# Setting the assumed lengths of ACT's units and TensorE's small jobs in a kernel that orders its own instructions

## The chip, the cores and the metric

The kernel runs on one core of a Trainium2 chip. The metric is the device time of one execution in microseconds (us). In the views below PE is TensorE's matmuls, PEld its weight loads, ACT is ScalarE, DVE is VectorE, POOL is GpSimd; L345 is line 345 of the kernel.

## The reference, cut to what matters

The program is an attention with pooled keys, and a two-layer network with a GELU of the quick kind behind it, on 49152 rows of 128:

```python
kv_pool = kv.reshape(B, H // 4, 4, W // 4, 4, C).mean(axis=(2, 4))
k = v = kv_pool.reshape(B, -1, C) @ w_sr           # 768 keys for each of 4 batches
s = (1.0 / np.sqrt(C)) * (q @ k.transpose(0, 2, 1))
a = softmax(s)                                       # exp of 49152 x 768 numbers
x = (a @ v).reshape(B * S, 128)
h = x @ w_in                                         # 128 -> 2048
g = h * (1.0 / (1.0 + np.exp(-1.702 * h)))           # 49152 x 2048 numbers
out = g @ w_out                                      # 2048 -> 128
```

## The kernel before

The kernel takes no scheduler's help: its Python code emits the instructions, and each engine runs its own in exactly that order. The work is cut into 700 *units*. A unit is a **fill** on PE (three matmuls of 512 columns into three PSUM banks) and one ACT instruction (exp or GELU) that turns those banks into a result in SBUF. Two sets of three banks alternate. Later, PE **drains** the results: for attention by matmuls of 129 columns (L345, twelve for a unit on average), for the network by output matmuls of 512 columns (L520, three for a unit). The results wait in a ring of 102 slots, three to a unit. Besides, PE has small jobs: pooling, making keys and values, transposes ("turns").

While it emits, the code keeps a reckoning of time in units of one 512-column matmul. `now` is PE's time, `end[n]` the time at which ACT ends unit n. Between two fills it emits drains and jobs as long as they fit ahead of the next fill, by these lengths:

```python
FIXED, CHUNK, SWITCH, HANDOVER, EVACUATE, LATE = 0.33, 1.975, 6.0, 1.0, 4.5, 1.0
COST = {pool_chunk: (2.5, 2.0), key_chunk: (0.7, 2.0), ...}    # PE's length, then time until the bank is free
SMALL, TURN = 0.26, 5.5                                        # SMALL: one 129-column matmul

def fill(p):
    ...                                                        # emits the fill and the ACT instruction
    begin = max(now + HANDOVER / 2, end[p - 1] if p else 0.0)
    ...                                                        # (cut) a switch of table adds SWITCH
    end.append(begin + FIXED + CHUNK * len(part))

for n in range(len(seq)):
    fill(n + 2)
    while True:
        room = room_ahead()                                    # free slots of the ring
        limit = end[-1] - K - HANDOVER                         # K = 3; (cut) no limit at the very end
        ...                                                    # small jobs, if they fit
        if not source:
            if todo_early and all(...made...):                 # parked exp units are all there
                source = todo_early
            else:
                source = todo
        ...
        cost = K * SMALL if kind == "a" else 1.0
        ...                                                    # (cut) drains whose results are not there yet
        start = now if source is todo_early else max(now, end[needs] + HANDOVER)
        ...                                                    # (cut) the first drain of a group waits for its bank
        if start + cost > limit and not (room < 2 * K + 1 or (room < 4 * K and start == now)):
            break                                              # (cut) the slot is full
        now = start + cost
        (drain_attn if kind == "a" else drain_moe)(i, c)
```

`room` counts the free slots of the ring. When fewer than 12 are free, a drain whose results are ready is emitted whether it fits or not, and when fewer than 7 are free, any drain is. I call this a **forced** drain, and "slot" with a length in us below means the PE work between the ends of two fills. Four of the attention groups ("early" or parked) have their exp made by DVE; their 24 chunks occupy a fixed part of the ring.

The softmax here doesn't subtract the row's maximum and nothing guards it: scores larger than these inputs give would overflow.

## Time and profile before

| what | value |
|---|---|
| time, three runs | 972.28, 972.39, 972.58 us |
| profiled execution | 971.47 us, span 969.7 us |
| PE busy, ACT busy | 946.0, 946.4 us (98% each) |
| first full ACT unit starts | 12.7 us |
| last ACT unit ends | 963.8 us |

A group's row in the profile reads: line, engine, operation, output and input with shapes, count, then busy time and mean length in ns of one, then the idle time just before them and what ended it. The groups of PE that the change's reckoning is about, by shape:

```profile
L520 PE MATMUL banks<-ag,w_out_sb 128*128 128x512 bf16 x1517 | 410.0, 379 | 1.8 <-ACT ag L515 0.5 <-DVE o_sb L528 0.2
L345 PE MATMUL banks<-v,ag 128*128 128x129 bf16 x2304 | 162.9, 220 | 0.4 <-DVE v L158 0.3
L134 PE MATMUL banks<-sum,x 128*128 128x32 bf16 x192 | 6.7, 177 | 0.1
```

The mean of one (379, 220, 177 ns) is not what a matmul costs, since each starts long before the previous record ends. What it costs is the distance from start to start. Some matmul records are missing in this trace (1517 of 1536 at L520).

### The profile page before, as it was taken

How to read it: one execution, taken by the hardware profiler on the slowest of the kernel's cores; microseconds unless marked ns; L12 is line 12 of the kernel's file. 1: busy time of each engine (PE TensorE's matmuls, PEld its weight loads, DVE VectorE, ACT ScalarE, POOL GpSimd, SP SyncE). 2: the span in 40 equal slices, each digit the busy share in tenths (PEclk: the TensorE clock that was granted, in tenths of full speed). 3: DMA queues.
4: the chain of work that ended last, by engine and by line, in shares of the span. 5: the costliest groups of instructions: out<-in, count | busy, mean ns of one | idle time of the engine just before them, and what ended most of it. 6: DMA issues, size and time to landing. Idle time of an engine off the chain costs nothing.

```text
span 969.7 us, 15127 instructions
## 1 busy us (share of the span) xinstructions
PE 946.0 (98%) x6244; PEld 504.7 (52%) x6359; DVE 344.0 (35%) x734; ACT 946.4 (98%) x705; POOL 65.7 (7%) x113
## 2 busy tenths in 40 slices
PE   7899999999999999999999999999999999999997
PEld 3567777544444444454445777754444444444443
DVE  4444433201477778777602333311111011011010
ACT  4999999999999999999999999999999999999997
POOL 3100100340000232000000000000000000000000
PEclk9999999999999999999999999999999999999999
DMA  9899841999862698224348994652222222222222
GB/s 182 161 201 148 110 96 34 108 147 172 162 130 44 103 149 110 41 34 76 57 81 132 182 174 106 131 120 40 37 44 39 38 44 34 43 34 40 37 33 43
DMA packets 354164, 89.66 MB, mean 92 GB/s; under 512 B 328048, under 2 KB 351728, under 8 KB 353776
## 3 DMA queue, kind: packets, MB, share of 16 engines
q1 hardware_dynamic: 323936, 56.06, 33.7%
q0 software_dynamic: 29104, 32.51, 22.6%
q8 instruction: 49, 0.80, 0.3%
q10 hardware_dynamic: 1056, 0.13, 0.1%
q14 instruction: 19, 0.16, 0.1%
HBM read 52.49 MB, written 45.88 MB: 101 GB/s over the span
## 4 chain that ended last, share of the span: by engine, by line
ACT 48%; PE 47%; DMA 3%; DVE 1%; issue 1%; POOL 0%; POOLq 0%
ACT ag L515 36%; PE banks L513 17%; PE banks L520 17%; ACT ag L336 13%; PE banks L345 6%; PE banks L334 5%; DMA qT<-q_bf 2%; DMA x<-in_q_dram 1%; DVE qT L230 1%; PE banks L382 1%; PE banks L424 0%; PE banks L224 0%; DVE o_sb L528 0%; ACT L515 0%; PE banks L134 0%
## 5 line engine op out<-in xcount | busy, mean ns | idle before, releaser
L515 ACT ACTIVATE ag<-banks 128x1536 bf16<-128x1536 f32 x512 | 690.0, 1543 | 1.6 <-PE banks L513 1.5
L513 PE MATMUL banks<-x,w_in_sb 128*128 128x512 bf16 x1484 | 411.2, 379 | 2.9
L520 PE MATMUL banks<-ag,w_out_sb 128*128 128x512 bf16 x1517 | 410.0, 379 | 1.8 <-ACT ag L515 0.5
L336 ACT ACTIVATE ag<-banks 128x1536 bf16<-128x1536 f32 (+1 forms) x188 | 250.6, 1445 | 12.2 <-PE banks L334 11.7
L520 PEld LDWEIGHTS <-w_out_sb 128*128 128x128 bf16 x1536 | 149.6, 97 | 181.7 <-issue 1.6
L513 PEld LDWEIGHTS <-w_in_sb 128*128 128x128 bf16 x1536 | 147.6, 97 | 176.5 <-issue 20.1
L528 DVE STREAM_TRANSPOSE o_sb<-banks 128x512 f32<-128x512 f32 x96 | 68.7, 716 | 398.8 <-PE banks L520 386.5
L345 PEld LDWEIGHTS <-ag 128*128 128x128 bf16 x2304 | 146.4, 98 | 45.4 <-issue 1.2
L345 PE MATMUL banks<-v,ag 128*128 128x129 bf16 x2304 | 162.9, 220 | 0.4 <-DVE v L158 0.3
L334 PE MATMUL banks<-qT,kT 128*128 128x512 bf16 x508 | 146.9, 379 | 9.3 <-ACT ag L336 4.8
L354 DVE RECIPROCAL rec<-banks 128x3 f32<-128x3 f32 x128 | 23.0, 180 | 132.9 <-PE banks L345 132.7
L409 DVE SCALAR_TENSOR_TENSOR ea<-ea,eb 128x512 f32<-128x512 f32 x96 | 65.9, 687 | 2.8
L334 PEld LDWEIGHTS <-kT 128*128 128x128 bf16 x552 | 47.4, 98 | 36.2 <-issue 4.5
L362 DVE TENSOR_TENSOR x<-banks,rec 128x384 bf16<-128x384 f32 x104 | 57.9, 557 | 3.6
L166 POOL DMA_DIRECT2D kvs<-in_kv_dram x32 | 40.4, 1319 | 15.8 <-DMA kvs<-in_kv_dram 11.6
L449 POOL MEMSET gate_tile<- 1x8 f32 x38 | 4.0, 106 | 461.9 <-DVE gate_tile L448 461.9
L398 DVE TENSOR_SCALAR ea<-banks 128x512 f32<-128x512 f32 x24 | 16.6, 691 | 30.1 <-PE banks L382 30.1
L411 DVE SCALAR_TENSOR_TENSOR ag<-ea,ee 128x512 bf16<-128x512 f32 x24 | 16.5, 686 | 1.0
L404 DVE SCALAR_TENSOR_TENSOR eb<-eb,ea 128x512 f32<-128x512 f32 x24 | 16.5, 688 | 0.7
L362 DVE TENSOR_TENSOR xt<-banks,rec 128x384 bf16<-128x384 f32 x24 | 13.4, 557 | 0.8
L230 DVE COPY qT<-banks 128x512 bf16<-128x512 bf16 x15 | 9.8, 686 | 4.8 <-PE banks L224 4.6
L426 DVE COPY x<-banks 128x768 bf16<-128x768 bf16 x12 | 6.7, 557 | 12.0 <-PE banks L424 11.9
(65 smaller groups left out, 154.5 us busy)
## 6 DMA issues: line engine op xcount, KB each, us to landing
out_dram<-o_sb SPq DMA_DIRECT2D x382, 64.0 KB, 2.0
kvs<-in_kv_dram POOLq DMA_DIRECT2D x32, 384.0 KB, 6.2
q_bf<-in_q_dram POOLq DMA_DIRECT2D x20, 512.0 KB, 7.3
x_bf<-x SPq DMA_DIRECT2D x13, 768.0 KB, 5.7
x<-in_kv_dram POOLq DMA_DIRECT2D x12, 512.0 KB, 12.3
x<-in_q_dram POOLq DMA_DIRECT2D x3, 512.0 KB, 20.6
w_in_sb<-in_moe_w_in_dram POOLq DMA_DIRECT2D x1, 512.0 KB, 5.1
w_out_sb<-in_moe_w_out_dram POOLq DMA_DIRECT2D x1, 512.0 KB, 6.6
```

The source lines that it names most:

```text
L166: nc.gpsimd.dma_start(out=kv_sums[b][:, i2], in_=kv_p[b, i, w, :, i2], **({"accum_op": ADD} if n else {}))
L230: nc.vector.tensor_copy(dst, src)
L334: nc.tensor.matmul(ps[:, k, :], kTs[i // GB][:, jc * 128:(jc + 1) * 128], rhs, start=True, stop=True)
L336: nc.scalar.activation(place([("a",) + c for c in chunks]), ps, AF.Exp, scale=scale)
L345: nc.tensor.matmul(av_of[u][:, k * (C + 1):(k + 1) * (C + 1)], weights(("a", i, jc))[:, o:o + T], vs[i // GB][:, jc, 0:C + 1], start=(jc = ...
L354: nc.vector.reciprocal(rec, ps[:, :, C])
L362: nc.vector.tensor_tensor(to, ps[:, :, 0:C], rec.unsqueeze(2).broadcast_to([128, TS, C]), MUL)
L409: nc.vector.scalar_tensor_tensor(a, a, COEFFS[k], b, ADD, MUL)
L513: nc.tensor.matmul(ps[:, k, :], w_in_sb[:, fc * 128:(fc + 1) * 128], x[:, g % (4 * XS) * G:(g % (4 * XS) + 1) * G], start=True, stop=True)
L515: nc.scalar.activation(place([("m",) + c for c in chunks]), ps, AF.Gelu_apprx_sigmoid)
L520: nc.tensor.matmul(o_of[g], w_out_sb[:, fc, :], weights(("m", g, fc)), start=(fc == 0), stop=(fc == FCH - 1))
L528: nc.vector.transpose(o_sb, o_of.pop(g))
```

## The change

Its intent is to put the lengths that an earlier trace shows in place of the old estimates. No instruction is added, removed or altered; only the order in which they are emitted follows from these numbers.

```diff
-    FIXED, CHUNK, SWITCH, HANDOVER, EVACUATE, LATE = 0.33, 1.975, 6.0, 1.0, 4.5, 1.0
-    COST = {pool_chunk: (2.5, 2.0), key_chunk: (0.7, 2.0), value_chunk: (0.7, 2.0),
-            transpose_q: (1.2, 4.0), early_fill: (1.0, 5.5), key_and_value: (1.0, 3.0),
-            transpose_pooled: (1.5, 3.0), make_k: (1.0, 3.0), make_v: (1.5, 3.0), turn: (1.5, 3.5)}
+    FIXED, CHUNK, SWITCH, HANDOVER, EVACUATE, LATE = 0.295, 1.978, 6.0, 1.0, 4.5, 1.0
+    COST = {pool_chunk: (1.9, 2.6), key_chunk: (0.3, 2.4), value_chunk: (0.3, 2.4),
+            transpose_q: (1.05, 4.2), early_fill: (1.0, 5.5), key_and_value: (0.55, 3.5),
+            transpose_pooled: (0.9, 3.6), make_k: (0.8, 3.2), make_v: (0.8, 3.7), turn: (1.55, 3.5)}
```

## The prediction

> **What bounds the kernel now.** I read the page's busy shares first, then ACT's waits, then ACT's groups in chosen stretches, then TensorE (PE) in order of time.
>
> ```profile
> PE 946.0 (98%) x6244; PEld 504.7 (52%) x6359; DVE 344.0 (35%) x734; ACT 946.4 (98%) x705; POOL 65.7 (7%) x113
> ```
>
> Both PE and ACT look full. The PE figure flatters: a matmul's record lasts 379 ns while the next starts after 216. ACT's figure also needs care, as shown below. ACT makes 700 units (up to three banks, 128x1536) of exp or GELU; nothing else can make them, except 24 chunks of exp on DVE. The waits of ACT over the whole run:
>
> ```profile
> ACT ag L336 <- PE banks L334: 11.7, 8, 3.9
> ACT qT L228 <- PE banks L224: 2.9, 1, 2.9
> ACT ag L515 <- PE banks L513: 1.5, 2, 1.3
> ```
>
> In order of time, almost all of the 11.7 us lies before 23 us (the first loads); the rest is 1.4 us near 39, 1.0 near 72.7 and 1.5 us near 425 to 428. So open idle time worth winning after the start is about 4 us. But some loss is not shown as idle. These are ACT's rows in five stretches, one answer each: 101 to 148, 152 to 230, 525 to 612, 641 to 803 and 850 to 960 us:
>
> ```profile
> L336 ACT ACTIVATE ag<-banks 128x1536 bf16<-128x1536 f32 x36 | 49.0, 1459 | 0.0
> L515 ACT ACTIVATE ag<-banks 128x1536 bf16<-128x1536 f32 x58 | 78.5, 1461 | 0.0
> L336 ACT ACTIVATE ag<-banks 128x1536 bf16<-128x1536 f32 x66 | 89.6, 1466 | 0.0
> L515 ACT ACTIVATE ag<-banks 128x1536 bf16<-128x1536 f32 x121 | 163.5, 1459 | 0.0
> L515 ACT ACTIVATE ag<-banks 128x1536 bf16<-128x1536 f32 x83 | 111.9, 1781 | 0.0
> ```
>
> The same instruction takes 1781 ns in the last row and about 1460 in the others. The records overlap, so I take the pace as (busy - one mean) / (count - 1): 1.358, 1.352, 1.356, 1.350 and 1.343 us per unit. My reading: 1.343 us is ACT's own pace; there its next unit is issued some 0.33 us early and queues behind the previous one, which the record includes. Where the mean is 1460 nothing queues: ACT starts each unit just when PE has filled the banks, and PE sets the pace, 7 to 15 ns per unit too slow, without any idle being shown.
>
> PE's pace is what the emitting code decides, because PE runs strictly in the order in which the code emits. Between two fills it places as much other work ("drains" and small jobs) as it believes fits in one ACT unit. Near 427 us it placed far too much:
>
> ```profile
> 424.66 0.81 PE L513 MATMUL banks<-x,w_in_sb 128*128 128x512 bf16 x2
> ...
> 425.31 1.18 PE L345 MATMUL banks<-v,ag 128*128 128x129 bf16 x18
> ...
> 426.33 1.24 PE L520 MATMUL banks<-ag,w_out_sb 128*128 128x512 bf16 x5
> ...
> 427.41 0.81 PE L513 MATMUL banks<-x,w_in_sb 128*128 128x512 bf16 x3
> ...
> 428.25 4.15 ACT L515 ACTIVATE ag<-banks 128x1536 bf16<-128x1536 f32 x3 [1.30 <-PE banks L513]
> ```
>
> Between two fills stand 18 attention matmuls and 5 output matmuls (one fill record is missing), 2.1 us of work; the ring of result slots was nearly full, and the code's rule for that case overrides the limit.
>
> **What the Trainium skill says.** "TensorE: Matmul & The Clock Gate", section "Wait — 56ns, not 53.3ns?", gives start-to-start times of warm matmuls of 215.7 ns at 512 columns, 55.6 at 128, and a floor of 25 for small ones. This trace agrees: x3 of 512 columns last 0.81 us, less one record of 0.379, over two steps: 0.215; x12 of 129 columns last 0.84, less 0.220, over 11: 0.056; sixteen 32-column ones last 0.55, less 0.177, over 15: 0.025. "Perfetto Trace Analysis", section "DVE / Act Engine Instruction", says the start that is reported is when an instruction leaves the execution queue for the ALUs; the 1781 ns means here speak against that for queued units, and I go by the trace. "ScalarE: Activation LUTs", section "What ACT_TABLE_LOAD costs", gives 186 ns + 0.833 per element less 93 of overlap, from which I estimate 1.373 us for 1536 elements; measured is 1.343, which decides.
>
> **The change part by part.** It adds and removes no instruction. The numbers steer the order alone; one unit of them is a 512-column matmul, 0.2157 us.
>
> (1) ACT's unit goes from 0.33 + 3 x 1.975 = 6.255 to 0.295 + 3 x 1.978 = 6.229, that is from 1.3492 to 1.3436 us. The new value is ACT's measured pace; the old one lets PE take 5.6 ns too much per unit, whenever there is a backlog of drains. That matches the 1.350 of the stretch from 641 us. In attention a triple of 129-column matmuls is reckoned at 0.78 but takes 3 x 0.0567 / 0.2157 = 0.789; 3.255 of drains is then 3.29, 6.29 in all, 1.357 us, as measured at 525 (1.356). After: 3.229 becomes 3.265, 1.351; this error of 1% stays, as the change leaves it alone.
>
> (2) The small jobs get shorter: sixteen pooling matmuls 16 x 0.0251 / 0.2157 = 1.86 (2.5 before, 1.9 now), two of 128 columns 0.52 (1.0, now 0.55), a turn of six 1.55 (1.5, now 1.55). Their sum with the time until the bank is free is about the same, so bank releases are not reckoned earlier. Effect: more drains beside a pooling job.
>
> The program order of both kernels, counted from fill to fill with the durations above, shows this. The first 27 slots are the same. Units 464 to 584 (641 to 803 us): 31 slots with four output matmuls become 28, mean work 1.3495 to 1.3441. Units 376 to 444 (second attention part): 1.3571 to 1.3522. Units 54 to 100 (first): 1.3558 to 1.3523. The backlog lasts longer: units 585 to 614, 1.3014 to 1.3445. The slots of 1.88 and 2.75 us near 425 us vanish; in their place one of 2.18 (27 attention matmuls, unit 309), one of 1.73 (321), and at 347 one of 1.98 instead of 1.63.
>
> Gains, counted in ACT units:
> - 641 to 816 us: 130 units at 1.350 become 1.344: 130 x 0.006 = 0.8 us.
> - 152 to 230 us: 57 units, of 0.009 lost about 0.007 comes back: 0.4.
> - Attention, 76 to 148 and 525 to 612 us: 47 + 65 units x 0.0057 = 0.6.
> - 232 to 418 us: 138 units, pace 1.344: 0.15 at most; I take 0.1.
> - The stall near 425: ends of ACT units are there 1.69 and 2.75 us apart instead of 1.343 each, 1.75 us lost, plus 0.17 at unit 347 (484 us). A slot costs its length less 1.343 less the lead that ACT has. In before the two slots exceeded by 1.94 and cost 1.75, the 1.63 one exceeded by 0.29 and cost 0.17; so the lead was 0.12 to 0.2, say 0.15. After: 2.18 costs 0.68, 1.73 costs 0.23, 1.98 costs 0.48: 1.4. Gain 1.92 - 1.4 = 0.5; with more lead (0.33, as late in the run) the gain is 1.1. I take 0.7.
> - 20 to 100 us: one slot of 1.66 becomes 1.33 (0.2 us lost at 48 us), but behind it stands a transposing transfer of q that lands at 71.8 and holds PE 1.1 us; what is won before is mostly waited out there. I take 0.1.
>
> Sum: 0.8 + 0.4 + 0.6 + 0.1 + 0.7 + 0.1 = 2.7 us. The start (23 us) and the tail after ACT's last unit (963.8 to 969.7) do not change. 972.4 - 2.7 = 969.7.
>
> **Rivals.** (a) A large gain, over 2%: it would need 19 us. ACT alone needs 700 units x 1.343 = 940 (a little less for eight shorter units), plus three table loads, plus 12.7 us until its first full unit and 6 of tail: about 961. What is left to win is some 10 us, of which 6 are start. I rule it out. (b) No gain: the lead is spent elsewhere. For it: the forced slots move rather than vanish, and the q transfer swallows early gains; against it: the pace in the 400 units is steady and set by the budget alone. It would leave 971.5 to 972.4. (c) A loss: with shorter job costs the code packs slots of 1.56 us (16 pooling and 9 attention matmuls) where before 1.39 stood, and holds the backlog longer, so the ring fills and other forced slots arise. For it: 2.18 at unit 309; against: the neighbours of the 1.56 slots hold 0.93 to 1.32. It could cost 1 to 2 us net, giving 973 to 974. (d) Transfers: loads issue where PE and DVE reach their gates, moved by a few units; a q transfer that lands 1 us later costs 1 us.
>
> **Range and chances.** The pace part (1.9 us) is firm to about 0.6; the forced slots and the transfers by about 1 each. I put 8 in 10 on 968.3 to 971.3. The runs of before lie within 0.3 us of each other, and 2% is 19.4 us: faster by over 2% 0.01, within 2% 0.98, slower 0.01.
>
> **What would show it.** ACT's pace from 641 to 803 falls from 1.350 to 1.343 to 1.345, its mean rises above 1459 ns; in attention it falls to about 1.351 with the mean still near 1460. The 1.3 us wait near 428 is gone, and one of 0.5 to 0.7 stands near 431. The q wait near 72 us stays around 1. Wrong would be: a pace unchanged at 1.350, new waits of ACT over 1 us, or PE waiting for DVE to free an accumulator.

## The result, and the profile after

The changed kernel took 968.87 us (median of 4 runs, 968.77 to 969.10); the kernel before took 972.49 (median of 4). The ratio is 0.9961, with an interval of 0.9944 to 0.9978. The predicted time was 969.7 with a range of 968.3 to 971.3. All outputs are right.

The two traces differ less than these medians: spans of 969.7 and 967.3 us, 2.4 us apart. In a later job both kernels ran on one chip in five rounds: 971.51 (median of 9) and 969.20 (median of 5), ratio 0.9973, 2.3 us apart. The earlier timed runs of before lay about 1 us above its own profiled execution (972.3 to 973.6 against 971.47). Those runs left no trace, so where that microsecond went stays open; I explain the 2.4 us that the traces hold.

The page's busy shares of the changed kernel, which tell next to nothing:

```profile
PE 950.7 (98%) x6359; PEld 505.5 (52%) x6359; DVE 345.2 (36%) x734; ACT 944.5 (98%) x705; POOL 65.7 (7%) x113
```

PE's count rises by 115 only because no record is missing in this trace. ACT's waits over the whole run, the three longest rows (engine, tile and line that waited, what it waited for, us in total, times, longest):

```profile
ACT ag L336 <- PE banks L334: 12.0, 8, 3.8
ACT qT L228 <- PE banks L224: 2.9, 1, 2.9
ACT ag L515 <- PE banks L513: 1.0, 2, 0.7
```

The waits fell by only 0.2 us in sum (11.7 + 1.5 to 12.0 + 1.0). A reader who judges by shown idle time would expect nothing. ACT's rows in the same five stretches as in the prediction show where the rest is:

```profile
L336 ACT ACTIVATE ag<-banks 128x1536 bf16<-128x1536 f32 x36 | 48.7, 1474 | 0.0
L515 ACT ACTIVATE ag<-banks 128x1536 bf16<-128x1536 f32 x59 | 79.5, 1470 | 0.0
L336 ACT ACTIVATE ag<-banks 128x1536 bf16<-128x1536 f32 x66 | 89.3, 1487 | 0.0
L515 ACT ACTIVATE ag<-banks 128x1536 bf16<-128x1536 f32 x122 | 164.1, 1483 | 0.0
L515 ACT ACTIVATE ag<-banks 128x1536 bf16<-128x1536 f32 x83 | 111.7, 1747 | 0.0
```

By (busy - one mean) / (count - 1):

| stretch, us | work | before | after |
|---|---|---|---|
| 101 to 148 | attention | 1.358 | 1.349 |
| 152 to 230 | end of attention's drains, then network | 1.352 | 1.345 |
| 525 to 612 | attention | 1.356 | 1.351 |
| 641 to 803 | network | 1.350 | 1.344 |
| 850 to 960 | network, no backlog | 1.343 | 1.341 |

The rows give busy time to 0.1 us, so each pace is good to 0.001 or 0.002; the difference in the last row is of that size. In the fourth stretch 122 units fit where 121 did.

The forced slot moved. PE's and ACT's instructions of the changed kernel in order of time (start, length, engine, line and operation, count, and in brackets the idle time before it and who ended it):

```profile
428.92 0.81 PE L513 MATMUL banks<-x,w_in_sb 128*128 128x512 bf16 x3
429.56 1.69 PE L345 MATMUL banks<-v,ag 128*128 128x129 bf16 x27
431.10 0.81 PE L513 MATMUL banks<-x,w_in_sb 128*128 128x512 bf16 x3
...
431.94 4.32 ACT L515 ACTIVATE ag<-banks 128x1536 bf16<-128x1536 f32 x3 [0.65 <-PE banks L513]
```

The wait of 1.30 us at 428 is gone, and one of 0.65 us stands at 432, behind 27 attention matmuls in one slot, as the program order had shown.

To account for every unit, I took from both traces the times at which ACT ends its units, and counted as loss what the distances exceed 1.3435 us, ACT's own pace. The shorter units of the start are counted at full length too, which makes the first row's loss some 4.2 us too small in both kernels and leaves its gain as it is. The losses are good to about 0.02 us. Units count from 0; a range a to b here and below runs from the end of unit a to the end of unit b:

| units | loss before, us | loss after, us | gain | gain predicted |
|---|---|---|---|---|
| 0 to 20, the start | 3.61 | 3.45 | 0.16 | 0 |
| 20 to 54 (40 to 88 us) | 1.89 | 1.89 | 0.00 | 0.1 |
| 54 to 101 and 376 to 446, attention | 4.30 | 3.63 | 0.67 | 0.6 |
| 101 to 262 | 0.67 | 0.13 | 0.54 | 0.5 |
| 262 to 350, forced slots | 1.97 | 1.79 | 0.18 | 0.7 |
| 446 to 590 | 0.88 | 0.09 | 0.79 | 0.8 |
| 590 to the end | 0.00 | 0.03 | -0.03 | 0 |

The attention row holds two loads of ACT's tables in both kernels; the range from 350 to 376, with the third, is left out: it loses 1.41 us in both. The sum is 2.3 of the 2.4 us.

### The profile page after: what moved, and what is told of

Its sections match the earlier page's. It is cut to its first block, busy times and chain, and to the rows that moved or that the text cites. A ratio compares the mean times of both kernels' runs of the same rounds, so it can differ in the third digit from the quotient of the medians.

```text
span 967.3 us, 15236 instructions
## 1 busy us (share of the span) xinstructions
PE 950.7 (98%) x6359; PEld 505.5 (52%) x6359; DVE 345.2 (36%) x734; ACT 944.5 (98%) x705; POOL 65.7 (7%) x113
## 4 chain that ended last, share of the span: by engine, by line
PE 50%; ACT 45%; DMA 3%; DVE 1%; issue 0%; POOL 0%; ACTq 0%; POOLq 0%
ACT ag L515 36%; PE banks L520 17%; PE banks L513 17%; ACT ag L336 9%; PE banks L345 7%; PE banks L334 7%; DMA qT<-q_bf 2%; DMA x<-in_q_dram 1%; DVE qT L230 1%; PE banks L382 1%; PE banks L224 0%; PE banks L424 0%; DVE o_sb L528 0%; ACT L515 0%; PE banks L134 0%
## 5 line engine op out<-in xcount | busy, mean ns | idle before, releaser
L515 ACT ACTIVATE ag<-banks 128x1536 bf16<-128x1536 f32 x512 | 688.9, 1539 | 1.2 <-PE banks L513 1.0
L334 PE MATMUL banks<-qT,kT 128*128 128x512 bf16 x552 | 149.7, 379 | 6.9 <-ACT ag L336 4.5
```

The source lines that it names most:

```text
L334: nc.tensor.matmul(ps[:, k, :], kTs[i // GB][:, jc * 128:(jc + 1) * 128], rhs, start=True, stop=True)
L515: nc.scalar.activation(place([("m",) + c for c in chunks]), ps, AF.Gelu_apprx_sigmoid)
```

## The experiments

All ran in two jobs of five rounds, on two chips, each with its own runs of the kernel before: 971.51 us in the first, 971.50 in the second (medians of 9). I therefore compare across the two jobs too, and give the change to 969.20, the changed kernel of the first job. The theory is that two separate things happen: PE's pace in backlogged stretches is the budget that the code gives it, and drains forced by a nearly full ring cost extra. Building the kept kernels again, without the chip, with a line that logs every drain gives the number of forced drains in each; I call that the emission log. It counts 14 in the kernel before (6 of them parked ones) and 22 in the changed one (5 parked).

### The changed kernel again

> The changed kernel itself, beside the others on one chip. Both theories: 3.6 us faster than before (3.0 to 4.0).

It took 969.20 us (968.89 to 969.73), ratio 0.9973 (0.9960 to 0.9985): 2.3 us faster than before, under the range that I had written down from the first result. Its trace repeats the first one: the losses of the rows above from unit 54 on agree within 0.02 us. The start and the wait for a transfer near 72 us vary more, by some 0.2 us each.

### Only ACT's unit

```diff
 # the kernel before, with
-    FIXED, CHUNK, SWITCH, HANDOVER, EVACUATE, LATE = 0.33, 1.975, 6.0, 1.0, 4.5, 1.0
+    FIXED, CHUNK, SWITCH, HANDOVER, EVACUATE, LATE = 0.295, 1.978, 6.0, 1.0, 4.5, 1.0
```

> Only ACT's unit is changed (6.255 to 6.229 matmul lengths), the small jobs keep the old costs. Program order from fill to fill: mean work in units 464 to 584 falls 1.3495 to 1.3441 us, as in the full change, but the two forced slots at units 304 and 305 (1.88 and 2.75 us) stay, with new ones of 1.73 and 1.71. My theory (two separate parts: the pace, and the forced slots): about 1.3 us faster than before (0.9 to 1.9), ACT's pace from 641 to 803 us 1.344, the wait of 1.3 us near 427 us still there. Rival (the small jobs' costs give all of the gain): at most 0.3 us faster and the pace still 1.350. Rival (luck of transfers): any value, with the same pace as before.

It took 970.64 us, ratio 0.9992 (0.9979 to 1.0005): 0.9 us by the medians, at the lower edge of what I expected, and not clear of noise as a time. The trace is clear. ACT's row from 641 to 803 us, and its longest wait in the network:

```profile
L515 ACT ACTIVATE ag<-banks 128x1536 bf16<-128x1536 f32 x121 | 162.8, 1477 | 0.0
```
```profile
ACT ag L515 <- PE banks L513: 1.8, 3, 1.3
```

The pace is (162.8 - 1.48) / 120 = 1.344, that of the full change, while the wait of 1.3 us is still there. From unit 446 to 590 it loses 0.17 us (before 0.88), but from 262 to 350 it loses 2.91 (before 1.97): less PE work per slot fills the ring sooner, and more is forced. The emission log bears this out: the ring is down to nine free slots at unit 224 (in before at 286, in the changed kernel at 309), and 46 drains are forced instead of 14. Part of the pace's gain is paid back there.

### Only the small jobs

```diff
 # the changed kernel, with
-    FIXED, CHUNK, SWITCH, HANDOVER, EVACUATE, LATE = 0.295, 1.978, 6.0, 1.0, 4.5, 1.0
+    FIXED, CHUNK, SWITCH, HANDOVER, EVACUATE, LATE = 0.33, 1.975, 6.0, 1.0, 4.5, 1.0
```

> Only the small jobs' costs are changed, ACT's unit stays 6.255. Program order: mean work in units 464 to 584 is 1.3495 as before; of the forced slots one of 2.10 us is left at unit 304 instead of 1.88 and 2.75. My theory: about 1.5 us faster than before (1.0 to 2.2), all of it near 425 us (about 1.2) and near 48 and 484 us, pace from 641 to 803 still 1.350. Rival (the unit alone matters): no gain. The two halves should add up to the whole change within 0.7 us.

It took 970.75 us, ratio 0.9989 (0.9977 to 1.0002): 0.8 us, less than I expected. Again the same two views, row and wait:

```profile
L515 ACT ACTIVATE ag<-banks 128x1536 bf16<-128x1536 f32 x121 | 163.5, 1457 | 0.0
```
```profile
ACT ag L515 <- PE banks L513: 0.8, 2, 0.5
```

The pace is (163.5 - 1.46) / 120 = 1.350, as before: the jobs' costs do nothing for it. From 262 to 350 it loses 0.65 us, 1.3 less than before, which is the gain that I expected there; the emission log has 7 forced drains. It lost 0.8 us between units 160 and 200, where before lost 0.04 and where I had expected nothing; the trace shows, among others, one output matmul that waited 0.4 us for DVE to empty the bank of a key job just before it (PE's wait between 215 and 300 us):

```profile
PE banks L520 <- DVE kT L186: 0.4, 1, 0.4
```

I had not looked for that in the program order. The halves sum to 1.6 us by the medians, against 2.3 for both, just within the 0.7 that I had allowed. From unit 54 on the traces give 0.9 and 0.5 against 2.2. What is missing is not in the forced slots: from 262 to 350 the unit alone loses 0.9 and the jobs alone win 1.3, 0.4 together, where both at once win 0.2. It lies between units 101 and 262: the unit alone wins 0.35 there, the jobs alone lose 0.70, but both at once win 0.55. So the jobs' new costs run into that loss only with the old unit; why, stays open.

### Parked drains only while the ring has room

```diff
 # the changed kernel, with
-                if todo_early and all((i, jc) in made ...
+                if todo_early and room >= 6 * K and all((i, jc) in made ...
```

> The changed kernel with one more condition: the parked exp units are drained only while at least 18 result slots are free. Theory: the forced slots come from draining those when fewer than 12 slots are free, since they free no slot; with the condition no slot over 1.6 us is left in the program order between units 102 and 356, the waits of ACT near 432 and 484 us vanish (0.72 + 0.17 + 0.47 us lost there in the changed kernel), so 1.3 us faster than the changed kernel (0.8 to 1.6), about 4.9 faster than before. Rival (the waits there come from DVE or from the q transfer at 431 us): the waits stay, same time as the changed kernel within 0.3 us.

It took 967.78 us, ratio 0.9960 (0.9946 to 0.9973), 1.4 us faster than the changed kernel beside it; 3.7 faster than before, where I had named 4.9 from the larger gap of the first measurement. All of ACT's waits that are left in this kernel:

```profile
ACT ag L336 <- PE banks L334: 11.8, 8, 3.8
ACT qT L228 <- PE banks L224: 3.1, 1, 3.1
ACT L228 <- PEq L719: 0.7, 1, 0.7
```

No row of L515 is left: the network's waits are gone. From unit 300 to 350 the loss falls from 1.57 us to 0.10. The emission log shows why: in the changed kernel, in the long slot of unit 309, nine slots were free, and five triples of *parked* attention drains were forced. The parked chunks keep their slots until the last is drained, so such a drain frees nothing, and output drains had to be forced right after (two in the next slot). With the gate, at least 12 slots stay free and not one drain is forced. The rival (DVE or a transfer of q at 431 us makes the wait) falls.

### The measured length of a 129-column matmul

```diff
 # the changed kernel, with
-    SMALL, TURN = 0.26, 5.5
+    SMALL, TURN = 0.263, 5.5
```

> The changed kernel with one more constant set to its measured length: a 129-column matmul reckoned at 0.263 instead of 0.26. Program order: mean work in the attention units 54 to 100 falls 1.3523 to 1.3451, 376 to 444 1.3522 to 1.3448; but a forced slot of 3.77 us stands at unit 305 instead of 2.18 and 1.73. Theory: attention wins 0.6 us or so (pace from 525 to 612 us 1.346), the forced slot loses about 0.7 more than the two of the changed kernel, 1.63 at 347 gives 0.35 back: the same as the changed kernel within 0.5 us. Rival (pace is all that counts): 0.8 us faster than the changed kernel.

It took 968.77 us, ratio 0.9976 (0.9964 to 0.9989): the same as the changed kernel. ACT's row in the stretch of 525 to 612 us, and its wait in the network:

```profile
L336 ACT ACTIVATE ag<-banks 128x1536 bf16<-128x1536 f32 x66 | 88.9, 1607 | 0.0
```
```profile
ACT ag L515 <- PE banks L513: 2.0, 1, 2.0
```

The mean of 1607 ns says that units now queue in front of ACT, and the pace is (88.9 - 1.61) / 65 = 1.343: attention is at ACT's own pace too. What this wins (0.7 us in the two attention ranges) went into a forced slot of 3.77 us: 2.08 us lost at units 300 to 310, 1.03 in the changed kernel. The 0.4 us between the medians is within the spread of the runs, so it is this slot, not the time, that speaks against the rival (pace is all that counts).

### Both

```diff
 # the changed kernel, with
-    SMALL, TURN = 0.26, 5.5
+    SMALL, TURN = 0.263, 5.5
-                if todo_early and all((i, jc) in made ...
+                if todo_early and room >= 6 * K and all((i, jc) in made ...
```

> Both: 0.263 and the parked exp drained only while 18 slots are free. Program order: attention 1.345, largest slot between units 102 and 356 is 1.73. Theory: the gains add: 2.2 us faster than the changed kernel (1.6 to 2.6), about 5.8 faster than before. Rival (late stretches take back what is won, since PE then is the bound overall): no more than 1.4 us faster than the changed kernel.

It took 966.59 us (966.38 to 967.19), ratio 0.9952 (0.9938 to 0.9965): 4.9 us faster than before, and 2.6 faster than the changed kernel, at the upper edge of what was expected. It beats both kernels. The 5.8 us against before that I had named came from the larger gap of the first measurement. ACT's row from 525 to 612 us:

```profile
L336 ACT ACTIVATE ag<-banks 128x1536 bf16<-128x1536 f32 x66 | 88.9, 1619 | 0.0
```

The gain in attention is as in the run before (1.343 per unit), and from 262 to 350 only 0.03 us is lost. Beyond 88 us, its three table loads aside (1.42 us each), it loses about 0.2 us in all against ACT's own pace.

### The budget too long, and too short

```diff
 # the changed kernel, with FIXED at 0.347 (unit_6281) or 0.28 (unit_6214)
-    FIXED, CHUNK, SWITCH, HANDOVER, EVACUATE, LATE = 0.295, 1.978, 6.0, 1.0, 4.5, 1.0
+    FIXED, CHUNK, SWITCH, HANDOVER, EVACUATE, LATE = 0.347, 1.978, 6.0, 1.0, 4.5, 1.0
```

> The changed kernel with ACT's unit reckoned 0.052 too long (6.281 matmul lengths, 1.3548 us) instead of right. Program order: attention 1.3668 and 1.3620, units 122 to 164 1.3544, units 464 to 584 only 1.3263 because the backlog is used up sooner; forced slots 1.73 and 1.66. Theory (PE's pace is set by the budget): the stretches 101 to 148 and 525 to 612 us run at 1.365 and 1.361 a unit; in all 3 to 4 us slower than the changed kernel. Rival (the drop of budget had no effect of its own): the same as the changed kernel within 0.5 us.

It took 972.58 us, ratio 1.0015 (1.0003 to 1.0028), 3.4 us slower than the changed kernel. The row from 525 to 612 us:

```profile
L336 ACT ACTIVATE ag<-banks 128x1536 bf16<-128x1536 f32 x65 | 88.6, 1460 | 0.1
```

That is (88.6 - 1.46) / 64 = 1.362 a unit, as expected. From 101 to 148 us it is 1.358 where I had named 1.365, a miss: before had 1.358 there too. Over the whole range from unit 54 to 101 it does lose more than before (2.38 us against 1.99); why this stretch did not follow its program order stays open. The rival (the budget has no effect of its own) falls.

> ACT's unit reckoned 0.015 too short (6.214, 1.3404 us). Program order: all stretches 1.340 to 1.349, so PE no longer sets the pace outside attention, but the drains fall behind and the forced slot at unit 305 grows to 3.77 us, with 1.80 at 347. Theory: the optimum of the budget is at ACT's pace; here 0 to 1 us slower than the changed kernel, with one ACT wait of about 2.2 us near 430 us. Rival (shorter is always better): 0.5 us faster.

It took 969.53 us, ratio 0.9981 (0.9969 to 0.9994), 0.3 us slower than the changed kernel, with one wait of 2.0 us from the slot of 3.77 us. ACT's row from 525 to 612 us:

```profile
L336 ACT ACTIVATE ag<-banks 128x1536 bf16<-128x1536 f32 x65 | 87.8, 1519 | 0.0
```

Attention ran faster, (87.8 - 1.52) / 64 = 1.348, and the ring took it back, 2.08 us at units 300 to 310. The 0.3 us is within the spread of the runs, so the times show only that the 0.5 us which "shorter is always better" had named did not come; the traces show where it went.

## Why the prediction was right

**What bounds the kernel.** Right: ACT's own pace is 1.343 us a unit. The runs with the length 0.263 brought attention to 1.343 and not lower, with the mean of a unit at 1607 to 1619 ns, so the mean's rise does mean that units queue there. In unit_6214 the network's program order allowed 1.340, and ACT still took (162.8 - 1.62) / 120 = 1.343 from 641 to 803 us. Two readings on the way were loose: of the 11.7 us of waits, 9.3 lie before 23 us, which is not almost all, and the 1.5 us near 425 belong to another row. And the floor of about 961 us in rival (a) is some 3 us too high, since the eight shorter units take 5.1 us less by their records (0.59 and 1.03 us instead of 1.45). Neither touches a term of the sum.

**Step (1), the budget sets PE's pace.** Right, and shown by the runs: pace 1.362, 1.356, 1.351 and 1.348 in the second attention stretch for units reckoned at 6.281, 6.255, 6.229 and 6.214 (6.255 with the old costs of the jobs, which the runs show to leave the pace alone), and in the network 1.350 or 1.344 by this number alone. Its predicted gains of 0.8, 0.4 and 0.1, and 0.6 us measured 0.79, 0.54 and 0.67. That SMALL's error of 1% keeps attention above ACT's pace is shown by the 0.263 run.

**Step (2), the small jobs.** Right that they leave the pace alone. I gave their effect as "more drains beside a pooling job" and did not see that they, more than the unit, shrink the forced slots (0.65 us lost and 7 drains forced with the jobs alone, 2.91 us and 46 with the unit alone).

**The forced slots.** The mechanism was right and the size off: this term of the sum was 0.7 us and measured 0.18. I gave ACT a lead of 0.15 us ahead of every long slot. The slot at unit 347 cost 0.47, as worked out (0.48), and the one at 321 only 0.04 instead of 0.23; but the one at 309 cost 0.76, with 0.17 more at the unit behind it and 0.09 from a smaller wait just before it, 1.03 in all instead of 0.68. And 0.23 us was lost at unit 298, where I had expected nothing. That slot holds four output matmuls (1.51 us), and the first of them waited for DVE to empty the bank of a value job:

```profile
414.60 1.02 PE L520 MATMUL banks<-ag,w_out_sb 128*128 128x512 bf16 x4 [0.24 <-DVE v L194]
```

This is the sign that I had named as one against me, PE waiting for DVE to free an accumulator. The prediction said that bank releases are not reckoned earlier; for this kind of job they are the same by the numbers (1.5 + 3.0 before, 0.8 + 3.7 now), but the order around it moved to where DVE was still busy with other work.

**The early stretch.** Right: the 0.2 us won at 48 us was waited out at the transfer of q, whose wait grew from 1.0 to 1.5 us on ACT (the prediction had it stay around 1); unit 44 ends at 74.2 us in both traces.

**The sum.** 2.7 us predicted, 2.4 in the traces, 2.3 in the paired job, 3.6 in the first measurement. The terms of pace came true one by one, so the sum is no luck. The base of 972.4 lay 0.9 us above the paired job's 971.5; from that base the same sum gives 968.8, so the hit does not rest on it. Of the rivals, (a) is refuted; (b) and (c) each describe a part (the early gain swallowed, the forced slots eating gains), but not the total. The slots of 1.56 us cost 0.14 us at one of their four places (unit 48) and almost nothing at the others. (d) was no more than 0.5 us.

## What to carry to other kernels

Where two engines are both near full, look for loss in the distance between the ends of the bounding engine's instructions, not in its idle time: an engine that gets each input just in time shows no idle time and still runs at another engine's pace (here 1.350 us a unit with 0.0 us idle, where its own pace was 1.343). In code that orders by reckoned lengths, an error of a fraction of a per cent in the bounding engine's length costs about that much in a stretch with a backlog (0.4% here: 5.6 ns reckoned, 6 measured in the network). But the right lengths only move the work, and a buffer that runs full can take the gain back elsewhere (0.7 us here with the length 0.263), so look there next. Work that frees no buffer should not be forced when buffers are short: not forcing it was worth 1.4 us here.

## What the Trainium skill lacked or had wrong

- "Perfetto Trace Analysis", section "DVE / Act Engine Instruction": it says the start that is reported is when an instruction leaves the execution queue for the ALUs. Here the same ACT instruction lasts 1450 ns when ACT had waited for it and up to 1788 ns when it queued, with ends 1.343 us apart, so the record of a queued one seems to include waiting behind the previous. A page could say that this mean tells a starved ACT from a bound one.
- "ScalarE: Activation LUTs", section "What ACT_TABLE_LOAD costs": the page's figures for immediate scale and bias (the kernel names no bias) lead to 1.373 us (an estimate) for back-to-back units of 1536 elements; measured is 1.343. Its 1283 ns for a table load agrees with the trace (1283). Its total of 2.66 us for a switch is more than is lost here: the ends of the units around the first load inside the run lie 2.76 us apart instead of 1.34, so the switch costs 1.42.
- "TensorE: Matmul & The Clock Gate", section "Back-to-back issue gap": the sustained 131 ns for 512 columns in a stream of weight load and matmul is not reached here, where each of such pairs takes 215 ns; that agrees with the page's 215.7 for back-to-back matmuls.
- No page speaks of reckoning lengths in code that orders its own instructions; the runs show 5.6 ns per unit of budget worth 6 ns per unit of pace.
